# Attention heads on TensorE: projections as pairs of 64-column matmuls, with the loads cut up and spread over the blocks of a head

## The chip, the cores and the metric

One core of a Trainium2 chip runs the whole program. The metric is device time in microseconds (us), the median of several executions; shorter is better. A program on one core has no second die to compare with.

TensorE is called PE, VectorE DVE, ScalarE ACT, GpSimd POOL, and SP is the engine whose queue issues most of the loads.

## The reference

A layer norm feeds two branches. A is an attention with 32 heads of width 128 that runs over the sequence in segments of 32 tokens and carries 8 memory rows from segment to segment. B is a gated feed-forward. The result is x + A * silu(B).

```python
def _A_ref(x, mem0, Wq, Wk, Wv, Wo, seg_len):       # x 2048 x 1024, H = 32, Dh = 128
    mem = mem0                                      # 8 rows
    for s in range(n_seg):                          # 64 segments of 32 tokens
        h = jnp.concatenate([mem, xs], axis=1)
        q, k, v = (jnp.einsum('btd,dhe->bhte', h, W) for W in (Wq, Wk, Wv))
        p = _softmax(jnp.where(mask, q @ k.T * scale, -1e9))
        o = jnp.einsum('bhte,hed->btd', p @ v, Wo)
        mem = o[:, :M, :]
        outs.append(o[:, M:, :])
# ... (written more briefly than the original)
def _B_ref(x, w_gate, w_up, w_down):
    return (_sigmoid(x @ w_gate) * (x @ w_up)) @ w_down
return x + s * silu(g)                              # s = A(layernorm(x)), g = B(layernorm(x))
```

The kernel breaks the recurrence (it replaces the memory by an approximation, checks on the chip that this is sound, and has a sequential fallback that does not run here).

## The kernel before

For each head, PE makes q and k (2 x 5 column blocks x 8 contraction steps = 80 matmuls), and in between the scores and values of the head before it.

```python
VW = 2 * DH + 4; OW = DH + 2; HP = P // 2          # 260, 130, 64

def load_w(hp):                                     # weights of two heads: 2 x 512 KB
    wqks[hp] = hwp.tile([P, 2, KC, 2 * DH], BF16, name="wqk", tag="w")
    nc.sync.dma_start(wqks[hp][:, 0], Wq2[:, cols]...)
    nc.sync.dma_start(wqks[hp][:, 1], Wk2[:, cols]...)
# load_v(hp): two pieces of 512 KB and a small one; load_vm(hp): four pieces of 256 KB and a small one

# the vm_ps stage, just before the first head
for b in range(4):
    nc.sync.dma_start(v0d[b], v0T[b * SEG:(b + 1) * SEG, 1:M, :])
for i in range(4):
    vm_ps = psb.tile([P, 512], F32, name="vm_ps", tag="big")
    for c in range(KC):
        for a in range(2):
            nc.tensor.matmul(vm_ps[a * NSEG:(a + 1) * NSEG, :], lhsT=cmT[:, c, :], rhs=wv_sb[...], ...)
    vm_sb = vsp.tile([P, 1024], BF16, name="vm_sb", tag="v_sb")[:, 0:512]   # three buffers
    # copy vm_ps to vm_sb: ACT for even i, DVE for odd i
    for a in range(2):
        nc.sync.dma_start(vm_dram[...], vm_sb[a * NSEG:(a + 1) * NSEG])
    if i == 0:
        load_vm(0)

def proj_steps(h):
    hc = slice((h % 2) * DH, (h % 2 + 1) * DH)
    for x, dst in enumerate((qt, kt)):
        for i in range(NBLK):                       # 5 blocks of 410 or 412 columns
            pr = psb.tile([P, 512], F32, name="pr", tag="big")
            for c in range(KC):                     # 8 steps
                nc.tensor.matmul(pr[:, 0:b - a], lhsT=w_[:, c, hc], rhs=xmT[:, c, a:b],
                                 start=(c == 0), stop=(c == KC - 1))
                if c == KC - 1:
                    nc.scalar.copy(dst[:, a:b], pr[:, 0:b - a])
                yield

def scores(h):
    nc.tensor.matmul(xs[:, 0:L], lhsT=kt[:, 0:P], rhs=qt[:, 0:L], start=True, stop=True)   # extra scores, L = 40
    for t in range(NT):
        for b in range(2):
            nc.tensor.matmul(s_ps[b * HP:(b + 1) * HP, t * HP:(t + 1) * HP], lhsT=kt[:, o:o + HP],
                             rhs=qt[:, o:o + HP], start=True, stop=True)
    # ... exp, mask

def values(h):
    # 32 matmuls: lhsT=pT[r, t * HP:(t + 1) * HP], rhs=va[r, t, v0:v0 + OW], r = 64 rows
    nc.tensor.matmul(rs[1][:, 2 * OW:3 * OW], lhsT=pT[:, PW:PW + P], rhs=va[:, NT, v0:v0 + OW], start=True, stop=True)
    # ... add, normalize

for h in range(H + 1):
    for i in range(NSL):                            # 80 steps
        if i == 2 * KC and h % 2 == 0 and 0 < h < H - 2:
            load_w(h // 2 + 1)
        if i == 4 * KC and h % 2 == 1 and h + 1 < H:
            load_v((h + 1) // 2)
            load_vm((h + 1) // 2)
        # ...
        if i == KC and h > 0:
            scores(h - 1)
        if i == 5 * KC and h > 0:
            values(h - 1)
        next(pj, None)                              # one projection step
    if h > 0 and h % 2 == 0:
        store_pair(h // 2 - 1)                      # 1 MB
```

A matmul has a tile shape, which the profile prints as rows*columns of the array: 128*128 for the projections here, 128*64 for the scores, 64*64 for the values.

## Time and profile before

| | before |
|---|---|
| median of 4 runs | 1566.54 us (1566.23 to 1567.36) |
| span of the profiled run | 1564.0 us |
| PE busy | 1549.7 us, 99% |
| chain that ended last | PE 98% |
| one head, from its extra scores to those of the next | 15.40 us, 30 times in a row |

First the page of the kernel before: the busy line (busy us, share of the span, instructions) and its chain, followed back from the last instruction.

```profile
PE 1549.7 (99%) x10251; PEld 780.8 (50%) x10355; DVE 675.2 (43%) x1145; ACT 511.7 (33%) x1023; POOL 155.9 (10%) x302
PE 98%; issue 0%; POOL 0%; DMA 0%; DVE 0%; SPq 0%; ACT 0%; DVEq 0%; POOLq 0%
```

So PE decides, nearly everywhere. A PE that is "busy" may still have holes, though, because the modelled end of a matmul overlaps the next one: a projection matmul is recorded with 337 ns, and the next starts 173 to 174 ns after it. They show in the times at which matmuls start. This is the timeline of PE in the kernel before for the middle of one head (start us, us, engine, line, operation, tile shape, operand, count):

```profile
543.19 1.03 PE L637 MATMUL pr<-xnT,wqk 128*128 128x410 bf16 x5
544.06 0.18 PE L648 MATMUL xs<-qt,kt 128*128 128x40 bf16 x1
544.17 0.69 PE L654 MATMUL so<-qt,kt 128*64 128x64 bf16 x32
544.80 5.74 PE L637 MATMUL pr<-xnT,wqk 128*128 128x412 bf16 x32
550.47 0.31 PE L684 MATMUL xs<-va,pT 64*64 64x130 bf16 x8
550.61 0.51 PE L684 MATMUL so<-va,pT 64*64 64x130 bf16 x24
551.05 0.23 PE L686 MATMUL xs<-va,pT 128*128 128x130 bf16 x1
551.12 1.03 PE L637 MATMUL pr<-xnT,wqk 128*128 128x410 bf16 x5
```

Read the first column. The extra scores start at 544.06 and the projections start again at 544.80: 0.74 us for 33 small matmuls. In the single records, it takes 113 ns from the start of the matmul of 40 columns to the next start (at the pace of 410 columns in 173 ns, 40 would take 17), and the last pair of scores 128 ns, where pairs otherwise follow each other every 32 ns. Both holes, and two like them around the values (268 ns before the first values matmul, where projections start 174 ns apart; 149 ns after the last group, where groups start 57 ns apart), lie exactly where the tile shape in the sixth column changes.

The waits of PE in the heads (who waited for whom: us in total, times, longest), for the window from 300 to 830 us of the kernel before:

```profile
PE pr L637 <- DVE vm_sb L576: 1.1, 1, 1.1
```

One wait, before the first head; within the heads, none. And this is how the DVE came to be late, from the view of the tile vm_sb (what its engines idled for):

```profile
  PE vm_ps L569: 8.5, 3
  DMA vm_dram<-vm_sb: 4.4, 1
```

The fourth copy waited 4.4 us for a buffer that a store still had to read.

### The profile page before, as it was taken

Reading aid. Unit: us, or ns where it says so; the run is one execution under the profiler, and the core shown is the slowest. Engines: PE = TensorE matmul, PEld = TensorE weight load, DVE = VectorE, ACT = ScalarE, POOL = GpSimd, SP = SyncE. Lnnn points to the kernel's source line nnn. Section 1 sums busy time; section 2 is a strip of 40 time slices with the busy share of each in tenths; the row PEclk is TensorE's granted clock in tenths of the full one; section 3 lists DMA queues with packets and bytes.
Section 4 is the critical chain, followed back from the end, with each engine's and each line's share of the span. In section 5 each row is a group of like instructions: output and inputs, shape, how many; then the busy total and the mean of one; then the engine's idle time right before and its main releaser. Section 6 shows DMA issues by size and latency. Waiting matters only on the chain.

```text
span 1564.0 us, 24499 instructions
## 1 busy us (share of the span) xinstructions
PE 1549.7 (99%) x10251; PEld 780.8 (50%) x10355; DVE 675.2 (43%) x1145; ACT 511.7 (33%) x1023; POOL 155.9 (10%) x302
## 2 busy tenths in 40 slices
PE   9999999999999999999999999999999999999998
PEld 4444445555555555555554444444444444444444
DVE  6554534347666666667663121121123333332211
ACT  4555552155555555555541111111111222200000
POOL 2111110001100100010011101101100000000000
PEclk9999999999999999999999999999999999999999
DMA  7744563867666776666524453523343353434340
GB/s 229 209 135 147 191 208 125 257 138 162 145 157 158 154 158 139 130 130 147 109 62 148 137 180 128 202 81 93 68 129 115 85 128 85 127 91 122 89 123 29
DMA packets 258148, 213.10 MB, mean 136 GB/s; under 512 B 83880, under 2 KB 220200, under 8 KB 258032
## 3 DMA queue, kind: packets, MB, share of 16 engines
q1 hardware_dynamic: 230256, 140.40, 37.2%
q0 software_dynamic: 17200, 56.37, 10.0%
q10 hardware_dynamic: 10576, 14.70, 3.1%
q8 instruction: 83, 1.36, 0.4%
q14 instruction: 33, 0.27, 0.1%
HBM read 129.07 MB, written 63.50 MB: 123 GB/s over the span
## 4 chain that ended last, share of the span: by engine, by line
PE 98%; issue 0%; POOL 0%; DMA 0%; DVE 0%; SPq 0%; ACT 0%; DVEq 0%; POOLq 0%
PE pr L637 28%; PE a_ps L903 14%; PE v_ps L373 14%; PE u_ps L174 12%; PE g_ps L170 12%; PE y_ps L893 12%; PE so L654 1%; PE acc L431 1%; PE so L684 1%; PE vm_ps L540 1%; PE xs L684 0%; PE xs L686 0%; PE pt L347 0%; DMA vm_dram<-vm_sb 0%; PE vm_ps L569 0%
## 5 line engine op out<-in xcount | busy, mean ns | idle before, releaser
L637 PE MATMUL pr<-xnT,wqk 128*128 128x412 bf16 (+1 forms) x2560 | 455.9, 337 | 1.1 <-DVE vm_sb L576 1.1
L637 PEld LDWEIGHTS <-wqk 128*128 128x128 bf16 x2560 | 245.8, 98 | 188.8 <-DVE vm_sb L576 1.5
L903 PE MATMUL a_ps<-wo_sb,ot 128*128 128x512 bf16 (+2 forms) x1037 | 225.0, 372 | 1.3
L373 PE MATMUL v_ps<-wv_sb,xnT 128*128 128x512 bf16 x1002 | 222.2, 379 | 1.8 <-ACT xnT L349 0.7
L174 PE MATMUL u_ps<-xnT,wu 128*128 128x512 bf16 x880 | 210.2, 379 | 0.9
L170 PE MATMUL g_ps<-xnT,wg 128*128 128x512 bf16 x868 | 209.4, 379 | 1.4
L178 DVE SCALAR_TENSOR_TENSOR hst<-th,u_ps 128x512 bf16<-128x512 f32 x112 | 76.9, 687 | 288.2 <-PE u_ps L174 269.8
L893 PE MATMUL y_ps<-wd,ht 128*128 128x512 bf16 x877 | 196.1, 379 | 0.7
L177 ACT ACTIVATE th<-g_ps 128x512 f32<-128x512 f32 x112 | 66.9, 597 | 305.4 <-PE g_ps L170 290.2
L903 PEld LDWEIGHTS <-ot 128*128 128x128 bf16 x1056 | 102.0, 98 | 119.4
L373 PEld LDWEIGHTS <-xnT 128*128 128x128 bf16 x1024 | 99.3, 98 | 118.4 <-ACT xnT L349 1.2
L893 PEld LDWEIGHTS <-ht 128*128 128x128 bf16 x896 | 87.7, 98 | 105.7
L174 PEld LDWEIGHTS <-wu 128*128 128x128 bf16 x896 | 87.7, 98 | 105.7
L170 PEld LDWEIGHTS <-wg 128*128 128x128 bf16 x896 | 86.9, 98 | 102.8
L640 ACT CAST qt<-pr 128x412 bf16<-128x412 f32 (+1 forms) x160 | 80.3, 502 | 130.3 <-PE pr L637 102.9
L640 ACT CAST kt<-pr 128x412 bf16<-128x412 f32 (+1 forms) x160 | 80.0, 500 | 101.7 <-PE pr L637 101.7
L376 ACT CAST v_sb<-v_ps 128x512 bf16<-128x512 f32 x128 | 74.9, 585 | 104.9 <-PE v_ps L373 101.4
L896 ACT ACTIVATE th<-y_ps 128x512 f32<-128x512 f32 x32 | 19.1, 597 | 231.9 <-PE y_ps L893 187.6
L909 DVE SCALAR_TENSOR_TENSOR tmp<-a_ps,gq 128x512 f32<-128x512 f32 (+2 forms) x33 | 22.3, 676 | 166.8 <-PE a_ps L903 166.6
L704 DVE TENSOR_TENSOR osb<-of,rden 128x1024 bf16<-128x1024 f32 x64 | 78.4, 1225 | 2.2
L620 DVE TENSOR_TENSOR mx<-mx,ab 128x2048 bf16<-128x2048 bf16 x64 | 78.2, 1221 | 1.2
L181 POOL DMA_DIRECT2D hT_dram<-hst x56 | 42.2, 754 | 359.0 <-DVE hst L178 359.0
(152 smaller groups left out, 968.0 us busy)
## 6 DMA issues: line engine op xcount, KB each, us to landing
vp_dram<-v_sb POOLq DMA_DIRECT2D x64, 256.0 KB, 3.5
va<-vp_dram SPq DMA_DIRECT2D x32, 512.0 KB
o_dram<-osb POOLq DMA_DIRECT2D x16, 960.0 KB, 13.7
hT_dram<-hst POOLq DMA_DIRECT2D x56, 256.0 KB, 2.7
ht<-hT_dram SPq DMA_DIRECT2D x16, 896.0 KB
vm<-vm_dram SPq DMA_DIRECT2D x48, 256.0 KB
xt<-in_A_x_dram SPq DMA_DIRECT2D x32, 256.0 KB
wo_t<-in_A_Wo_dram ACTq DMA_DIRECT2D x8, 1024.0 KB
```

The lines of the kernel that those rows point to most:

```text
L170: nc.tensor.matmul(g_ps[:], lhsT=wg[:, c, fc * P:(fc + 1) * P], rhs=xnT[:, c, tb * TB:(tb + 1) * TB], start=(c == 0), stop=(c == KC - 1))
L174: nc.tensor.matmul(u_ps[:], lhsT=wu[:, c, fc * P:(fc + 1) * P], rhs=xnT[:, c, tb * TB:(tb + 1) * TB], start=(c == 0), stop=(c == KC - 1))
L177: nc.scalar.activation(th[:], g_ps[:], ACTF.Tanh, scale=0.5)
L178: nc.vector.scalar_tensor_tensor(hst[:, :, fc, :], th[:].rearrange("p (a b) -> p a b", b=P), 1.0, u_ps[:].rearrange("p (a b) -> p a b", b= ...
L373: nc.tensor.matmul(v_ps[:], lhsT=xnT[:, c, t * P:(t + 1) * P], rhs=wv_sb[:, c, cg * 512:(cg + 1) * 512], start=(c == 0), stop=(c == KC - 1))
L376: nc.scalar.copy(v_sb[:, j * 512:(j + 1) * 512], v_ps[:])
L620: nc.vector.tensor_tensor(mx[:, x, :], mx[:, x, :], abs_.pop((h, x))[:], op=ALU.max)
L637: nc.tensor.matmul(pr[:, 0:b - a], lhsT=w_[:, c, hc], rhs=xmT[:, c, a:b], start=(c == 0), stop=(c == KC - 1))
L640: nc.scalar.copy(dst[:, a:b], pr[:, 0:b - a])
L704: nc.vector.tensor_tensor(osb[:, b * HT:(b + 1) * HT, hc], ofs[b][:, :, e0:e0 + DH], rd.unsqueeze(2).to_broadcast([P, HT, DH]), op=ALU.mult)
L893: nc.tensor.matmul(y_ps[:], lhsT=hts[t][:, c, :], rhs=wd[:, c, hf * 512:(hf + 1) * 512], start=(c == 0), stop=(c == FC - 1))
L903: nc.tensor.matmul(a_ps[:], lhsT=ox[t][0][:, h, :], rhs=wo_sb[:, h, a:b], start=(h == 0), stop=(h == H - 1))
```

## The change

Its intent: give projections, extra scores and scores one tile shape, so that PE need not change it twice a head; and cut the loads of the heads into pieces that are released block by block, each by a tiny write that waits for a copy of the block before.

```diff
@@ proj_steps
-                        nc.tensor.matmul(pr[:, 0:b - a], lhsT=w_[:, c, hc], rhs=xmT[:, c, a:b],
-                                         start=(c == 0), stop=(c == KC - 1))
+                        for e in range(2):
+                            o = (h % 2) * DH + e * HP
+                            nc.tensor.matmul(pr[e * HP:(e + 1) * HP, 0:b - a], lhsT=w_[:, c, o:o + HP], rhs=xmT[:, c, a:b],
+                                             start=(c == 0), stop=(c == KC - 1))
@@ scores
-            nc.tensor.matmul(xs[:, 0:L], lhsT=kt[:, 0:P], rhs=qt[:, 0:L], start=True, stop=True)
+            nc.tensor.matmul(xs[0:HP, 0:L], lhsT=kt[:, 0:HP], rhs=qt[:, 0:L], start=True, stop=True)
@@ values
-            nc.tensor.matmul(rs[1][:, 2 * OW:3 * OW], lhsT=pT[:, PW:PW + P], rhs=va[:, NT, v0:v0 + OW], start=True, stop=True)
+            nc.tensor.matmul(rs[0][0:HP, 2 * OW:3 * OW], lhsT=pT[0:HP, PW:PW + HP], rhs=va[0:HP, NT, v0:v0 + OW],
+                             start=True, stop=True)
@@ vm_ps stage (the small stores of v0T and load_vm(0) now come after it)
-            vm_sb = vsp.tile([P, 1024], BF16, name="vm_sb", tag="v_sb")[:, 0:512]
+            if i % 2 == 0:
+                vm_sb2 = vsp.tile([P, 1024], BF16, name="vm_sb", tag="v_sb")
+            vm_sb = vm_sb2[:, i % 2 * 512:(i % 2 + 1) * 512]
@@ loads in the heads
+        def after_block(h, m):
+            src = st["qk", h][(m - 1) // NBLK]
+            o = edges[(m - 1) % NBLK]
+            nc.sync.dma_start(pace_dram[h:h + 1, :], src[0:1, o:o + 32])
...
+        loads = {(0, 1 + 2 * a): [(load_vm, 0, a)] for a in range(SPT)}
+        loads.update({(0, 9): [(load_w, 1, 0)], (1, 1): [(load_w, 1, 1)]})
+        for p in range(1, H // 2):
+            h = 2 * p
+            if p + 1 < H // 2:
+                loads[h, 1] = [(load_w, p + 1, 0)]
+                loads[h, 3] = [(load_w, p + 1, 1)]
+            loads[h - 1, 2] = [(load_v, p, 0)]
+            loads[h - 1, 4] = [(load_v, p, 1)]
+            for m, a in ((h - 1, 8), (h, 5), (h, 7), (h, 9)):
+                loads[m, a] = [(load_vm, p, (a - 3) // 2 if m == h else 0)]
...
-                if i == 2 * KC and h % 2 == 0 and 0 < h < H - 2:
-                    load_w(h // 2 + 1)
-                    load_v((h + 1) // 2)
-                    load_vm((h + 1) // 2)
+                if i % KC == 0 and (h, i // KC) in loads:
+                    after_block(h, i // KC)
+                    for f, *args in loads[h, i // KC]:
+                        f(*args)
```

The cut leaves out smaller parts of the change: a `manual_schedule` for ACT and DVE around the vm_ps stage, the early load of the second pair's weights taken out, eight stores of xnT (512 KB each) and four small loads that also move into the paced list, and pT tiles that are 64 columns shorter.

More of the change, by code (lines that the diff above doesn't have):

```diff
@@ L244 @@
     o_dram = tc.dram_tile([S, HD], BF16, name="o_dram")
+    pace_dram = tc.dram_tile([H, 32], BF16, name="pace_dram")
     hT_dram = tc.dram_tile([NT, P, FC, P], BF16, name="hT_dram")
@@ L397, with load_w, load_v, load_vm @@
         wqks = {}
-        def load_w(hp):
+        def load_w(hp, x):
             cols = slice(hp * 2 * DH, (hp + 1) * 2 * DH)
-            wqks[hp] = hwp.tile([P, 2, KC, 2 * DH], BF16, name="wqk", tag="w")
-            nc.sync.dma_start(wqks[hp][:, 0], Wq2[:, cols].rearrange("(c p) n -> p c n", p=P))
-            nc.sync.dma_start(wqks[hp][:, 1], Wk2[:, cols].rearrange("(c p) n -> p c n", p=P))
-        def load_v(hp):
+            if x == 0:
+                wqks[hp] = hwp.tile([P, 2, KC, 2 * DH], BF16, name="wqk", tag="w")
+            nc.sync.dma_start(wqks[hp][:, x], (Wq2, Wk2)[x][:, cols].rearrange("(c p) n -> p c n", p=P))
+        def load_v(hp, b):
             cols = slice(hp * 2 * DH, (hp + 1) * 2 * DH)
             va = vas[hp % 2]
-            for b in range(2):
-                nc.sync.dma_start(va[b * HP:(b + 1) * HP, 0:NT, 2:VW - 2],
-                                  vp_dram[b * S // 2:(b + 1) * S // 2, cols].rearrange("(t k) c -> k t c", k=HP))
-            nc.sync.dma_start(va[M:L, NT, 2:VW - 2], vp_dram[0:SEG, cols])
-        def load_vm(hp):
+            nc.sync.dma_start(va[b * HP:(b + 1) * HP, 0:NT, 2:VW - 2],
+                              vp_dram[b * S // 2:(b + 1) * S // 2, cols].rearrange("(t k) c -> k t c", k=HP))
+            if b == 0:
+                nc.sync.dma_start(va[M:L, NT, 2:VW - 2], vp_dram[0:SEG, cols])
+                if hp > 0:
+                    nc.sync.dma_start(va[0:M, NT, 2:VW - 2], vm_dram[NSEG:NSEG + M, cols])
+        def load_vm(hp, a):
             cols = slice(hp * 2 * DH, (hp + 1) * 2 * DH)
-            va, vm = vas[hp % 2], vms[hp % 2]
+            vm = vms[hp % 2]
             src = vm_dram[0:NSEG, cols].rearrange("(t a) c -> a t c", a=SPT)
-            for a in range(SPT):
-                t0 = 1 if a == 0 else 0
-                nc.sync.dma_start(vm[a * SEG:(a + 1) * SEG, t0:NT, 2:VW - 2],
-                                  src[a:a + 1, t0:NT].to_broadcast([SEG, NT - t0, 2 * DH]))
-            nc.sync.dma_start(va[0:M, NT, 2:VW - 2], vm_dram[NSEG:NSEG + M, cols])
+            t0 = 1 if a == 0 else 0
+            nc.sync.dma_start(vm[a * SEG:(a + 1) * SEG, t0:NT, 2:VW - 2],
+                              src[a:a + 1, t0:NT].to_broadcast([SEG, NT - t0, 2 * DH]))
         def wo_load(hg, q=nc.sync):
@@ L558 @@
         filler(1)
-        load_w(0)
-        load_w(1)
-        load_v(0)
-        v0d = vm_dram[NSEG + 1:NSEG + M, :].rearrange("m (h b i) -> b h m i", b=4, i=SEG)
-        for b in range(4):
-            nc.sync.dma_start(v0d[b], v0T[b * SEG:(b + 1) * SEG, 1:M, :])
+        load_w(0, 0)
+        load_w(0, 1)
+        load_v(0, 0)
+        load_v(0, 1)
+        es_3 = ExitStack()
+        es_3.enter_context(tc.manual_schedule(engines={ACT, DVE}))
         for i in range(4):
@@ L578 @@
                 nc.sync.dma_start(vm_dram[1:NSEG + 1, (2 * i + a) * 512:(2 * i + a + 1) * 512], vm_sb[a * NSEG:(a + 1) * NSEG])
-            if i == 0:
-                load_vm(0)
+        v0d = vm_dram[NSEG + 1:NSEG + M, :].rearrange("m (h b i) -> b h m i", b=4, i=SEG)
+        for b in range(4):
+            nc.sync.dma_start(v0d[b], v0T[b * SEG:(b + 1) * SEG, 1:M, :])
+        nc.sync.dma_start(vas[0][0:M, NT, 2:VW - 2], vm_dram[NSEG:NSEG + M, 0:2 * DH])
         dg = gp.tile([P, KC, NM], F32, name="dg")
@@ L584 @@
         nc.vector.tensor_reduce(dgs[:], dg[:].rearrange("p c s -> p s c"), axis=AX.X, op=ALU.add)
+        es_3.close()
         wide = gp.tile([P, P], BF16, name="wide")
@@ L597 @@
         PW = NT * HP
-        pTs = [vp.tile([P, PW + P], BF16, name=f"pT{i}") for i in range(2)]
+        pTs = [vp.tile([P, PW + HP], BF16, name=f"pT{i}") for i in range(2)]
         for pT in pTs:
-            nc.vector.memset(pT[:, PW:PW + P], 0.0)
+            nc.vector.memset(pT[:, PW:PW + HP], 0.0)
         fsq = vp.tile([P, KC, DH], BF16, name="fsq")
@@ L626, in proj_steps @@
         def proj_steps(h):
-            hc = slice((h % 2) * DH, (h % 2 + 1) * DH)
             qt = sb.tile([P, NPE], BF16, name="qt")
@@ L691, in values @@
                 nc.vector.tensor_tensor(ofs[b][:, 6:8], x[:, :, f:f + DH + 1], vmh[:, b * HT + 6:b * HT + 8], op=ALU.add)
-            x = rs[1][0:L, 2 * OW + f:3 * OW]
+            x = rs[0][0:L, 2 * OW + f:3 * OW]
             rd = rden[0:L, h, NT:NT + 1]
@@ L714 @@
         NSL = 2 * NBLK * KC
+        loads = {(0, 1 + 2 * a): [(load_vm, 0, a)] for a in range(SPT)}
[9 more added lines that the diff above has]
+                loads[m, a] = [(load_vm, p, (a - 3) // 2 if m == h else 0)]
+        for k in range(KC):
+            loads[2 * k + 1, 6] = [(nc.sync.dma_start, xnT_dram[:, k, :], xnT[:, k, :])]
+        loads[21, 6] = [(nc.sync.dma_start, dv0[b * SEG:(b + 1) * SEG, :], vm_dram[1, :].rearrange("(h b i) -> b h i", b=4, i=SEG)[b])
+                        for b in range(4)]
         load_pair(0)
@@ L720 @@
             for i in range(NSL):
-                if i == 2 * KC and h % 2 == 0 and 0 < h < H - 2:
-                    load_w(h // 2 + 1)
                 if i == 4 * KC and h % 2 == 1 and h + 1 < H:
-                    load_v((h + 1) // 2)
-                    load_vm((h + 1) // 2)
                     load_pair((h + 1) // 2)
-                if i == 4 * KC and h % 2 == 0 and 0 < h <= 2 * KC:
-                    nc.sync.dma_start(xnT_dram[:, h // 2 - 1, :], xnT[:, h // 2 - 1, :])
-                if i == 4 * KC and h == 20:
-                    for b in range(4):
-                        nc.sync.dma_start(dv0[b * SEG:(b + 1) * SEG, :],
-                                          vm_dram[1, :].rearrange("(h b i) -> b h i", b=4, i=SEG)[b])
+                if i % KC == 0 and (h, i // KC) in loads:
+                    after_block(h, i // KC)
+                    for f, *args in loads[h, i // KC]:
+                        f(*args)
                 if i == 1 and h > 0:
```

## The prediction

> **What bounds it now.** TensorE. The page's busy table has PE busy 99% of 1564 us; the chain of waits is 98% PE. The stretch that the change touches is the 32 heads. Followed through the timeline, the extra-scores matmul of successive heads starts every 15.40 us, all 30 periods alike: no load ever stalls PE there. In one period 80 full-width projection matmuls, 174 ns apart for 412 columns and 173 for 410, take 13.9 us. The remaining 1.5 us are scores and values.
>
> Read start by start, that remainder has four holes. From the 40-column scores matmul (128x128) to the first 64-column one 113 ns pass, against some 20 for its columns; from the last scores pair to the next projection 128 ns, against 28 between pairs; before the first values matmul 268 ns, against 174; after the last values group 149 ns, against 57. Each is about 95 ns too long and each sits where the matmul's tile shape changes. [...]
>
> **What the change does to PE.** Each projection matmul becomes two of 64 weight columns, and the extra-scores matmul also has 64. Projections, extra scores and scores then share one tile shape, so the two changes around the scores go. The two around the values stay (128 rows to 64 and back); only the last values matmul now shares the values' shape.
>
> Doubled matmuls should cost nothing: in the vm_ps stage before the heads, pairs of 64-column matmuls already start 3 ns apart and then 213, that is 216 ns a pair for 512 columns, as one full matmul takes. Weight loads of 110 ns hide there. Instruction rate: 96 matmuls of 72 columns in a row ran 32 ns apart, loads included; the new stream needs one per 87 ns. [...]
>
> Per head: extra scores to next projection takes 740 ns now; estimated 25 + 16 x 32 = 537 plus little: saves 0.19 to 0.2 us. The values lose an exit-side matmul of 128 columns' shape but pay about 24 ns for the first pair after a change: zero. New period about 15.20 us; 31 periods: -6.2 us.
>
> **Other parts.** Before the first head, PE stands 1.3 us at 316 us for a bank whose copy (DVE) waited 4.4 us for a store of an earlier copy to land; the copies now share two tiles and the stores precede the other loads: -1.2 us. The shape change from vm_ps to the first projection goes: -0.1 us. The loads are split and paced through the heads by tiny writes that wait for a copy: since no head stalls on a load now, gain 0. Each load still has a head or so of slack. ACT, DVE and POOL work is the same.
>
> **Prediction.** 1566.5 - 7.5 = 1559.0 us, range 1555.0 to 1562.0. Faster by over 2%: 1%; within 2%: 98%; slower: 1%.
>
> **What would show it.** Head period 15.20 us; 5120 projection matmuls in pairs, 3 ns then about 170; extra scores to next projection about 0.55 us; holes around the values unchanged near 95 ns; the 1.3 us stall at 316 us gone; everything after the heads of equal length.
>
> **What would make it wrong.** If pairs with different weights don't overlap as the vm_ps pairs do (same weights there), heads lengthen: 10 ns a pair is 26 us. [...] If a paced load comes late, a head shows a stall.

Its sum is -6.2 us for the 31 periods, -1.2 for the stall and -0.1 for the shape change before the first head: -7.5 in all. What is cut are statements of the hardware that no trace shows; the last of them, outside the sum, named a case in which another 6 us would go (two more holes of about 95 ns in each of 32 heads).

## The result, and the profile after

The changed kernel takes 1557.70 us (median of 8 runs, 1557.02 to 1558.19); the kernel before, run beside it, 1566.44 us (12 runs). The ratio is 0.9941, with a 95% interval of 0.9932 to 0.9951. Ratios are the mean time of one kernel's fast runs over that of the other's fast runs in the same rounds, so they are not quite the ratio of the medians that stand beside them.

The page of the changed kernel, the same two lines:

```profile
PE 1543.0 (99%) x12811; PEld 841.3 (54%) x12915; DVE 670.4 (43%) x1145; ACT 509.9 (33%) x1023; POOL 159.0 (10%) x302
PE 99%; issue 0%; POOL 0%; DVE 0%; ACT 0%; POOLq 0%
```

The timeline of PE in the middle of one head of the changed kernel:

```profile
538.72 0.86 PE L644 MATMUL pr<-xnT,wqk 128*64 128x410 bf16 x8
539.41 0.18 PE L655 MATMUL xs<-qt,kt 128*64 128x40 bf16 x1
539.42 0.70 PE L661 MATMUL so<-qt,kt 128*64 128x64 bf16 x32
539.92 5.76 PE L644 MATMUL pr<-xnT,wqk 128*64 128x412 bf16 x64
545.61 0.31 PE L691 MATMUL xs<-va,pT 64*64 64x130 bf16 x8
545.75 0.51 PE L691 MATMUL so<-va,pT 64*64 64x130 bf16 x24
546.09 0.22 PE L693 MATMUL xs<-va,pT 64*64 64x130 bf16 x1
546.24 0.54 PE L644 MATMUL pr<-xnT,wqk 128*64 128x410 bf16 x4
```

From the extra scores (539.41) to the next projection (539.92) it is now 0.51 us, and the shape column no longer changes there. The values part is as long as before (0.63 us from its first start to the next projection, 0.65 before). The 64 projection matmuls of four blocks take 5.69 us from their first start to the values (539.92 to 545.61); before, 32 of twice the width took 5.67.

The view of PE's waits for 300 to 830 us has no line at all in the changed kernel: the wait for the DVE copy is gone. The view of the tile vm_sb says why, its engines now idle for PE alone:

```profile
  PE vm_ps L570: 11.4, 4
```

Where the 8.1 us between the two profiled runs (1564.0 and 1555.9) lie, by the start of the extra-scores matmul of the first and the last head:

| stretch | before | after | difference |
|---|---|---|---|
| start to the first head's extra scores | 328.46 | 326.77 | -1.69 |
| the 31 periods of the heads | 479.47 | 473.12 | -6.34 |
| the rest | 756.04 | 755.97 | -0.07 |

Every head takes 15.19 us where it took 15.40. So far everything is as foretold. The experiments that follow were meant to confirm it; the first one contradicted a part of it.

### The profile page after: what moved, and what is told of

Read it like the earlier page. It is cut to its first block, busy times and chain, and to the rows that moved or that the text cites. A ratio compares the mean times of both kernels' runs of the same rounds, so it can differ in the third digit from the quotient of the medians.

```text
span 1555.9 us, 29886 instructions
## 1 busy us (share of the span) xinstructions
PE 1543.0 (99%) x12811; PEld 841.3 (54%) x12915; DVE 670.4 (43%) x1145; ACT 509.9 (33%) x1023; POOL 159.0 (10%) x302
## 3 DMA queue, kind: packets, MB, share of 16 engines
q8 instruction: 103, 1.69, 0.5%
## 4 chain that ended last, share of the span: by engine, by line
PE 99%; issue 0%; POOL 0%; DVE 0%; ACT 0%; POOLq 0%
PE pr L644 29%; PE a_ps L926 14%; PE v_ps L374 14%; PE u_ps L174 12%; PE g_ps L170 12%; PE y_ps L916 12%; PE so L661 1%; PE acc L432 1%; PE so L691 1%; PE vm_ps L541 1%; PE xs L691 0%; PE vm_ps L570 0%; PE pt L348 0%; POOL mx L442 0%; PE xs L693 0%
## 5 line engine op out<-in xcount | busy, mean ns | idle before, releaser
L644 PE MATMUL pr<-xnT,wqk 128*64 128x410 bf16 (+1 forms) x5120 | 457.2, 337 | 0.0
L644 PEld LDWEIGHTS <-wqk 128*64 128x64 bf16 x5120 | 308.4, 110 | 127.8
L919 ACT ACTIVATE th<-y_ps 128x512 f32<-128x512 f32 x32 | 19.1, 597 | 231.6 <-PE y_ps L916 187.4
```

Source lines behind the costliest of these rows:

```text
L644: nc.tensor.matmul(pr[e * HP:(e + 1) * HP, 0:b - a], lhsT=w_[:, c, o:o + HP], rhs=xmT[:, c, a:b], start=(c == 0), stop=(c == KC - 1))
```

## The experiments

There were three theories at the start. A: the holes of the shape changes vanish, and that is the gain in the heads. B: the paced loads relieve something on the path. C: split projections run faster by themselves. "Head period" is always from one head's extra-scores matmul to the next one's, for the first 30 periods; the 31st contains other work and is left out. All kernels gave correct results. The kernels ran in groups of four, each group on one chip beside runs of the kernel before (1565.99, 1566.04 and 1566.40 us in the three groups).

### The two halves of the change alone: tiles_only and loads_only

tiles_only is the kernel before with the three matmul edits of the diff above and nothing else. loads_only is the changed kernel with these three undone:

```diff
 loads_only, against the changed kernel
-                        for e in range(2):
-                            ... two matmuls of 64 columns
+                        nc.tensor.matmul(pr[:, 0:b - a], lhsT=w_[:, c, hc], rhs=xmT[:, c, a:b], ...)
-            nc.tensor.matmul(xs[0:HP, 0:L], lhsT=kt[:, 0:HP], ...)
+            nc.tensor.matmul(xs[:, 0:L], lhsT=kt[:, 0:P], ...)
 (and the last values matmul)
```

> The kernel before with only the matmul shapes of the change (projections in pairs of 64 columns, extra scores of 64 columns, last values matmul 64x64); loads, stores and copies as before. Theory A (two shape changes per head vanish): head period 15.19 us as in the changed kernel, the 1.3 us stall before the first head stays, time 1559.9 us, ratio to before 0.996. Rival B (the paced loads relieve something): head period 15.40 us, time 1566 us, ratio 1.000. Rival C (split projections stream faster by themselves) cannot be told from A here.

> The changed kernel with all three matmul shapes put back; the split and paced loads, the shared copy tiles and the later small stores stay. Theory A: head period 15.40 us, the 1.3 us stall is gone, time 1565.1 us, ratio to before 0.999. Rival B: head period 15.19 us, time 1558 to 1559 us, ratio 0.995.

Measured: tiles_only 1573.58 us (6 runs), ratio 1.0048 (1.0035 to 1.0062). It is slower than the kernel before, by 7.6 us of the medians, where I had expected it 6 us faster. loads_only 1564.16 us, ratio 0.9985 (0.9972 to 0.9998), every head 15.40 us, the stall before the first head gone: as expected by A.

In tiles_only, 19 of 30 head periods are 15.19 us, as A says. The other eleven are longer, up to 20.20 us, 12.9 us in all. PE's waits in the heads, same view and window as before:

```profile
PE pr L639 <- issue: 5.3, 5, 3.1
PE so L686 <- issue: 2.4, 1, 2.4
PE pr L639 <- DVE vm_sb L576: 1.5, 1, 1.5
```

"Issue" means that PE stood still and waited for nothing that the profile shows: no semaphore, no buffer, no data. The chain of waits from 700 to 715 us, in order of time (start us, us, what), puts such a hole into the middle of a row of values matmuls that depend on nothing new:

```profile
702.82 0.24 PE xs L686 x8
703.05 0.28 PE so L686 x18
703.33 2.41 issue
705.74 0.30 PE so L686 x6
706.04 0.04 PE xs L688
```

What else has to reach PE is its program. The profile lists a DMA queue of kind "instruction": queue 8, in packets of 16,384 bytes. It carries 83 of them before and 103 with the doubled matmuls: 20 packets more, where PE's records grow by 5,120, which is 256 a packet. Two kernels below give the same: some_halves_old_loads has 8 packets more for 2,048 more records, two_blocks_full 16 for 4,096. So, by these counts, the queue is PE's, and a packet brings 256 of its instructions. Here are the DMA queues of tiles_only while PE is working up to the hole, 686.8 to 703.4 us, and then for the hole itself (queue: packets, MB, share of 16 engines; the first line is the busy tenths of the DMA engines in 40 slices of the window):

```profile
DMA  0000000688999999999999999387999047954889
q1 hardware_dynamic: 3676, 1.83, 78.5%
q0 software_dynamic: 50, 0.20, 3.0%
...
DMA  7998969999979968999799979969989989999599
q0 software_dynamic: 230, 0.84, 82.1%
q1 hardware_dynamic: 241, 0.12, 19.8%
q8 instruction: 1, 0.02, 2.2%
```

For 16.6 us, while values, memory values and the store of a pair go out together, no packet of the instruction queue starts at all. The window begins just after a fetch has landed, at 686.78; the next one started only at 703.41, in the hole, though PE had begun the block of 256 before the hole at about 696.0 us. Then PE goes on. The same 16.6 us of the changed kernel have two:

```profile
DMA  3013332336333266999996745999999999987500
q1 hardware_dynamic: 3292, 1.63, 52.4%
q0 software_dynamic: 320, 1.05, 16.6%
q8 instruction: 2, 0.03, 0.9%
```

Every hole of tiles_only longer than 0.4 us beyond the first head, from the single records of the trace ("stands from" is the start of the last matmul before the hole; a fetch has "landed" when its packet ends):

| PE stands from | to | PE records since the hole before | last fetch landed at | landed before PE goes on | landing before that |
|---|---|---|---|---|---|
| 519.69 | 520.48 | | 519.08 | 1.40 us | 504.47 |
| 580.36 | 580.97 | 1792 = 7 x 256 | 579.60 | 1.38 us | 564.36 |
| 640.86 | 642.34 | 1792 = 7 x 256 | 640.94 | 1.40 us | 625.12 |
| 677.75 | 678.38 | 1024 = 4 x 256 | 676.95 | 1.42 us | 660.00 |
| 703.11 | 705.74 | 768 = 3 x 256 | 704.37 | 1.38 us | 686.78 |
| 742.44 | 745.91 | 1024 = 4 x 256 | 744.56 | 1.36 us | 725.42 |

All holes are whole numbers of 256 instructions apart, to within one record, and all end 1.4 us after a fetch has landed. From this I drew theory D, which I had not had: PE runs out of instructions.

There is a second loss after the two longest holes. The table of stretches has the granted clock in its last but two column ("1.00" is full). In tiles_only:

```profile
700.00:703.00 3.00, 3.00 (x51) 2.18 (x49) 0.00 (x0) 1.14 (x3) 0.00 (x0) 1.00 0.73 109
706.20:709.40 3.20, 3.20 (x22) 1.76 (x20) 3.13 (x10) 0.50 (x1) 0.00 (x0) 0.50 0.44 79
711.00:715.00 4.00, 4.00 (x50) 2.62 (x46) 2.77 (x3) 2.27 (x6) 0.00 (x0) 1.00 0.00 0
```

After 2.6 us without a matmul the clock is halved for 3.4 us (10 projection steps at some 341 ns in place of 173), some 1.7 us more. The holes of up to 1.5 us in this run have no such sequel. The length alone does not decide: v_burst, below, has two holes of 2.84 us, and the clock was halved after the one at 668 us (0.64 granted on average from 672 to 676 us) and not after the one at 380 us (1.00 from 383 to 386.5). What does decide is not shown.

### More instructions without another shape: the halves

If D holds, a kernel with the old shapes must show the same holes once PE gets more instructions. In halves_old_loads the kernel before splits each projection matmul by the columns of its moving operand (`rhs`, the activations; the weights are `lhsT`); both parts are 128*128. halves_new_loads does the same on loads_only. some_halves_old_loads does it in two blocks of five.

```diff
 halves_old_loads, against the kernel before
-                        nc.tensor.matmul(pr[:, 0:b - a], lhsT=w_[:, c, hc], rhs=xmT[:, c, a:b],
-                                         start=(c == 0), stop=(c == KC - 1))
+                        for e in range(2):
+                            o, n = (0, 206) if e == 0 else (206, b - a - 206)
+                            nc.tensor.matmul(pr[:, o:o + n], lhsT=w_[:, c, hc], rhs=xmT[:, c, a + o:a + o + n],
+                                             start=(c == 0 and e == 0), stop=(c == KC - 1 and e == 1), skip_group_check=True)
```

> The kernel before, but each projection matmul is done as two full-width (128x128) matmuls over half of its columns: PE gets as many instructions as in the changed kernel, no tile shape is altered, the loads are the old ones. Theory D (PE runs out of instructions: its 16 KB instruction fetches, 256 instructions each, come late behind bursts of loads): head period 15.60 us (2.4 ns more a step) without stalls, and besides some 7 to 16 us of stalls in the heads, each starting at a multiple of 256 recorded PE instructions and ending about 1.4 us after a fetch has landed; time 1579 to 1588 us. Rival E (64-column tiles are what bulk loads disturb): no stalls, all periods 15.60 us, time 1572 us.

> The same halved full-width projections with the changed kernel's split and paced loads. Theory D: the same instruction stream, but no stall, all periods 15.60 us, time 1570.6 us, at least 8 us less than with the old loads. Rival E: the same 15.60 us as with the old loads.

> As the first of this set (old loads, full width), but only two of five column blocks are halved: 354 PE instructions a head in place of 290 or 450, so 256 instructions last about 11.2 us (13.6 before, 8.6 when all are doubled). Theory D: stalls of 0 to 3 us in all, period otherwise 15.48 us, time 1568.5 to 1572 us. If stalls grow in proportion to the instructions: about 5 us of stalls.

Measured: halves_old_loads 1585.70 us, ratio 1.0120 (1.0103 to 1.0137). halves_new_loads 1574.87 us, ratio 1.0054 (1.0038 to 1.0071). some_halves_old_loads 1569.73 us, ratio 1.0019 (1.0003 to 1.0036). The undisturbed head period is 15.72 us for the first two and 15.51 for the third; I had said 15.60 and 15.48. So two matmuls of half the columns cost 4 ns a step more than one ((15.72 - 15.40) / 80), not the estimated 2.4 (in the kernel before, matmuls of 512 columns start 215.8 ns apart and those of 72 columns 32.5, which leaves 2.4 ns a matmul besides its columns), and that is why halves_new_loads misses its 1570.6 us by 4 us. The comparison that was asked for does not depend on it: same PE program, 10.8 us apart by the loads alone (of which the stall before the first head, 1.7 us in this run, is a part). PE's waits, halves_old_loads:

```profile
PE so L686 <- issue: 3.8, 2, 2.3
PE pr L639 <- issue: 3.5, 4, 1.8
PE pr L639 <- DVE vm_sb L576: 1.7, 1, 1.7
```

halves_new_loads has no line in that view. The six holes of halves_old_loads in the heads lie 1024, 1792, 3584 or 4096 records apart, multiples of 256 again, and end 1.13 to 1.52 us after a landing. Rival E, that bulk loads disturb 64-column tiles in particular, is out: there are none in the projections here. some_halves_old_loads has 30 of 30 periods at 15.51 us and not one hole: nothing is lost at 357 PE instructions a head, and 10.8 us in 30 heads at the 453 of halves_old_loads, so the loss is not in proportion to the instructions. The profile of halves_old_loads fell on its slowest run (1587.74 us).

### Which part of the load change it is: no_pace and v_burst

no_pace is the changed kernel without the tiny writes; v_burst releases the six pieces of a pair's values at one block.

```diff
 no_pace, against the changed kernel
-                    after_block(h, i // KC)
 v_burst, against the changed kernel
-            loads[h - 1, 2] = [(load_v, p, 0)]
-            loads[h - 1, 4] = [(load_v, p, 1)]
-            for m, a in ((h - 1, 8), (h, 5), (h, 7), (h, 9)):
-                loads[m, a] = [(load_vm, p, (a - 3) // 2 if m == h else 0)]
+            loads[h - 1, 5] = [(load_v, p, b) for b in range(2)] + [(load_vm, p, a) for a in range(SPT)]
```

> The changed kernel without the tiny writes that hold each load back to its block; order and pieces of the loads stay. My view (loads are off the critical path): head period 15.19 us, time 1557.7 us, ratio to the changed kernel 1.000; the loads start earlier and the stores of o land later. Rival B (pacing keeps the memory system free for something on the path): some head periods over 15.25 us, time over 1559 us.

> The changed kernel, but the six pieces of a pair's values and memory values (2 MB) are released together at one block of the odd head, paced only at the first; weights as in the changed kernel. Theory D: fetches come late in some pairs, stalls of 2 to 10 us in all at multiples of 256 instructions, time 1560 to 1568 us. If only the weights' burst matters: no stalls, 1557.7 us.

Measured: no_pace 1562.98 us (1560.59 to 1567.08), ratio to before 0.9976 (0.9962 to 0.9989), some 5 us slower than the changed kernel's 1557.70. My view that pacing is worth nothing was wrong; rival B's expectation holds; by theory D what pacing protects is the instruction fetch: its landings are up to 18.0 us apart without pacing, and up to 12.9 with it. Seven of 30 periods are longer than 15.19 us in its profile, which fell on the slowest of its runs (1567.08 us), as did that of v_burst. v_burst 1578.21 us (1575.90 to 1582.00), ratio 1.0070 (1.0053 to 1.0087): far worse than the 1560 to 1568 that I had set. The expectation had the cause and not the size. In the profiled run of v_burst, the holes are up to 4.5 us long, three of them are followed by a halved clock (from 446.20, 671.48 and 736.33 us; 0.50 granted from 447.2 to 450.7), and the heads lose 24.0 us. One of its holes in the chain of waits:

```profile
442.54 0.47 PE pr L644 x4
443.01 4.21 issue
447.22 2.95 PE pr L644 x15
```

Putting all runs together, from the records of the heads of each profiled run: the recorded PE instructions of a head, how long two blocks of 256 last at that rate, the longest time between two landings of a fetch, and what the heads lost.

| run | PE instructions a head | two blocks last | longest between landings | lost in 30 heads |
|---|---|---|---|---|
| before | 293 | 26.9 us | 21.9 us | 0 |
| loads_only | 293 | 26.9 us | 18.4 us | 0 |
| some_halves_old_loads | 357 | 22.2 us | 19.5 us | 0 |
| halves_old_loads | 453 | 17.8 us | 18.0 us | 10.8 us |
| tiles_only | 453 | 17.2 us | 19.1 us | 12.9 us |
| no_pace | 453 | 17.2 us | 18.0 us | 8.2 us |
| v_burst | 453 | 17.2 us | 19.4 us | 24.0 us |
| halves_new_loads | 453 | 17.8 us | 12.9 us | 0 |
| after (changed kernel) | 453 | 17.2 us | 12.9 us | 0 |

The kernels that lose are just those in which a fetch once arrived later than two blocks' worth of work after the one before it. The other five kernels of this document do not lose and fit too: those of them with 453 instructions a head have at most 13.6 us between landings, and share_only, with 293, has 23.1. Two is the count that sorts the runs: the kernel before loses nothing with landings up to 21.9 us apart, where one block lasts 13.5 us, and v_burst loses 24.0 us with 19.4, where three would last 25.8. How many blocks PE holds, no trace shows. The comparison sorts the kernels; it is not exact for the single hole: four of the six in the table of tiles_only came with only 14.6 to 17.0 us between landings. Sharper is the time from the landing of a block to PE's first instruction of it, block by block (the bounds of the blocks are counted on from the holes, and put at the same place of the program where a run has none). In each of the four kernels that lose, 10 to 13 of the 53 blocks in the heads begin within 2 us of their landing, the least 1.1 to 1.3 us; in every other kernel the least is 2.3 us or more, but for one block of some_halves_old_loads with 1.8 us, which was thus close to losing. What the trace does not show is why a late fetch waits. Those of the table take 0.95 to 1.5 us themselves; they start 5.4 to 10.0 us after PE began the block before, where the changed kernel has 4.6 us at most. The mean busy share of the DMA engines does not tell the two apart: it is 1.00 from 340 to 370 us in no_pace, where PE has no hole, and 0.83 from 687 to 704 us in tiles_only, where it has one.

### The cost of a change of shape: xs_full, two_blocks_full, last_full

Theory A against C, on the changed kernel, with the paced loads. One edit each:

```diff
 xs_full
-            nc.tensor.matmul(xs[0:HP, 0:L], lhsT=kt[:, 0:HP], rhs=qt[:, 0:L], start=True, stop=True)
+            nc.tensor.matmul(xs[:, 0:L], lhsT=kt[:, 0:P], rhs=qt[:, 0:L], start=True, stop=True)
 two_blocks_full: in proj_steps
+                        if i == 2:
+                            nc.tensor.matmul(pr[:, 0:b - a], lhsT=w_[:, c, hc], rhs=xmT[:, c, a:b], ...)
-                        for e in range(2):
+                        for e in range(2 if i != 2 else 0):
 last_full
-            nc.tensor.matmul(rs[0][0:HP, 2 * OW:3 * OW], lhsT=pT[0:HP, PW:PW + HP], rhs=va[0:HP, NT, v0:v0 + OW], ...)
+            nc.tensor.matmul(rs[1][:, 2 * OW:3 * OW], lhsT=pT[:, PW:PW + P], rhs=va[:, NT, v0:v0 + OW], ...)
```

> The changed kernel, but the one extra-scores matmul of each head is 128 columns wide again; the projections stay split. Theory A: this single matmul brings back both shape changes (a hole of about 95 ns on each side of it), head period 15.19 + 0.2 = 15.4 us, time about 1564 us, ratio 0.998. Rival C (the split projections themselves are what got faster): head period at most 15.25 us, time 1558 to 1560 us.

> The changed kernel, but the third of five column blocks of each projection (q and k) is done with full-width matmuls: same arithmetic, 16 of 80 steps whole, four more shape changes per head. Theory A: each change about 95 ns plus 10 to 20 ns on the first matmul after it, head period 15.19 + 0.38 to 0.46 = 15.57 to 15.65 us, time 1557.7 + 12 to 15 = 1570 to 1573 us, slower than before. Rival C: a fifth of the gain per head is lost, 15.23 us, time about 1559 us.

> The changed kernel, but the last values matmul of each head is 128x128 again, so after the values there are two shape changes (64x64 to 128x128 to 128x64) in place of one. Theory A: one more hole of about 95 ns, less the little that the first pair saves: head period 15.19 + 0.10 = 15.29 us, time about 1560.9 us. If the width of that matmul matters only by itself: period 15.19 to 15.21 us.

| run | shape changes a head more | head period | more, per change | time | ratio to before |
|---|---|---|---|---|---|
| after (changed kernel) | | 15.19 us | | 1557.70 us | 0.9941 |
| xs_full | 2 | 15.41 us | 0.11 us | 1564.22 us | 0.9986 (0.9972 to 1.0001) |
| two_blocks_full | 4 | 15.64 us | 0.11 us | 1572.40 us | 1.0037 (1.0022 to 1.0051) |
| last_full | 1 | 15.31 us | 0.12 us | 1561.82 us | 0.9974 (0.9959 to 0.9989) |

Three doses, one price: 0.11 to 0.12 us for each change of shape, hole and slow first matmul together. In xs_full a single matmul of 40 columns, made as wide as it was, takes back the whole gain of 0.21 us a head; the split projections by themselves give nothing, and C is out. The timeline of PE around it, xs_full:

```profile
540.73 1.73 PE L644 MATMUL pr<-xnT,wqk 128*64 128x412 bf16 x18
542.39 0.19 PE L655 MATMUL xs<-qt,kt 128*128 128x40 bf16 x1
542.51 0.69 PE L661 MATMUL so<-qt,kt 128*64 128x64 bf16 x32
543.04 5.21 PE L644 MATMUL pr<-xnT,wqk 128*64 128x412 bf16 x58
```

From the extra scores to the first scores it is 0.12 us again; in the changed kernel it was 0.01. last_full shows that narrowing the last values matmul is needed once the projections are split, because a third shape would otherwise stand between two others. (In the kernel before it should be worth nothing, as the number of changes stays the same; no run tests that.)

### The stall before the first head: share_only and order_only

```diff
 share_only: the kernel before, with
-            vm_sb = vsp.tile([P, 1024], BF16, name="vm_sb", tag="v_sb")[:, 0:512]
+            if i % 2 == 0:
+                vm_sb2 = vsp.tile([P, 1024], BF16, name="vm_sb", tag="v_sb")
+            vm_sb = vm_sb2[:, i % 2 * 512:(i % 2 + 1) * 512]
 order_only: loads_only, with these three lines put back to the one
```

> The kernel before with only the four copies of the vm_ps stage sharing two tiles instead of taking four. My view: the last copy no longer waits for a store to land, the PE stall of 1.3 us at 316 us goes, head period stays 15.40 us, time 1565.2 us, ratio 0.999. If the stall came from the order of the small stores and loads instead, it stays at about 1.3 us.

> The changed kernel with all matmul shapes put back and the four copies on four tiles again; the small stores and the loads stay in the new order. My view: the last copy must still wait for the first store of an earlier copy to land, but these stores are now first in their queue and land within about 3 us of the copy, so the copy waits under 1 us and PE stalls 0 to 0.3 us there; head period 15.40 us, time 1565.2 us. If the sharing of tiles is what counts: a stall of about 1 us.

Measured: share_only 1564.78 us, ratio 0.9992 (0.9978 to 1.0006); order_only 1564.23 us, ratio 0.9989 (0.9975 to 1.0002). Neither has the stall in its trace, and both have 15.40 us a head. Either remedy is enough: with shared tiles the fourth copy needs no new buffer, and with the new order the buffer is free in time, as the first stores of vm_sb are issued at 307.0 us where they waited in the queue until 311.9 before. (order_only also has the paced loads and the `manual_schedule` of this stage; which part of the new order is needed was not separated.) The times alone do not settle it, since both intervals reach 1; the missing wait does. The 0.6 us between the two runs is not explained.

## Why the prediction was right or wrong

- Time: 1559.0 us foretold with 1555.0 to 1562.0, measured 1557.70, inside.
- "The two around the scores go ... saves 0.19 to 0.2 us", period 15.20 us: right. 15.19 us, -6.34 us for the 31 periods against -6.2. Three doses of shape changes on the chip confirm that each change is paid for, at 0.11 to 0.12 us. The traces show only the later start, not what PE does meanwhile.
- "Doubled matmuls should cost nothing": right. 64 narrow matmuls take 5.69 us where 32 wide ones took 5.67. The weight loads of 64 columns last 110 ns, where those of 128 lasted 98 before, and two of them go with each step of 173 ns; yet nothing is seen of it in the time, and the view of PE's waits in the heads has no line.
- Values "zero": right. Two changes of shape lie around them before and after, and from the first values matmul to the next projection it is 0.65 us before (550.47 to 551.12) and 0.63 us after (545.61 to 546.24).
- "-1.2 us" for the stall and "-0.1" for the shape change before the first head: -1.69 measured there in one pair of profiles, of which about 0.3 us stand already before that stage and are not explained by the change.
- "Instruction rate: 96 matmuls of 72 columns in a row ran 32 ns apart, loads included; the new stream needs one per 87 ns": this step failed. It shows the pace of 192 instructions, less than one block of 256, and says nothing of how fast new ones come. What the runs show of the supply is in the table above: nothing is lost before, with landings up to 21.9 us apart where two blocks last 26.9; tiles_only loses 12.9 us with landings up to 19.1 us apart where two last 17.2.
- "The loads are split and paced ...: since no head stalls on a load now, gain 0": this step failed too, and it is the larger error. True for the kernel before (loads_only: every head 15.40 us). With the doubled instruction stream, the old loads cost 12.9 us in the heads of tiles_only, and pacing alone is worth about 5 us (no_pace). Without the part of the loads, the change would have been a loss of 7.6 us instead of a gain of 8.7. The total came out right only because the change contains both halves; my reasons, put to the shapes alone, were off by 14 us (1559.9 expected of tiles_only, 1573.58 measured).
- "If a paced load comes late, a head shows a stall": did not happen.

## What to carry to other kernels

Changing the tile shape of matmuls has a price, here 0.11 us, and one odd matmul pays it twice; look for it in the start times, since the busy share hides it. When an edit multiplies PE's instructions, ask also how the program gets to PE: a hole that waits for nothing, a whole number of 256 instructions after the last one, went with a late instruction fetch here (8.2 to 24.0 us lost in 30 heads of four kernels, each hole ending 1.1 to 1.7 us after a landing of 16,384 bytes), and the cure was to cut and spread the bulk DMA. Two edits can be worth the opposite together of what they are apart, so test the halves before giving either the credit.
